# First unit of a chunked delta rule ahead of an MLP: scores times solved values directly behind T times v, corner products in pieces, SyncE's loads behind T

## The chip, the cores and the metric

The kernel runs on one core of a Trainium2 chip. The metric is the device time of one execution in microseconds; three executions were timed, and one more was profiled. PE is TensorE, DVE is VectorE, ACT is ScalarE, POOL is GpSimd, SP is SyncE, which here only issues DMAs.

## The reference

Two stages: a delta rule over 768 tokens for 4 batches and 8 heads (head size 48), then an MLP with a squared ReLU over the 3072 rows that it gives.

```
k_n = k / (norm(k) + 1e-6)
for t in range(S):
    y[:, :, t] = q_t @ state
    v_old = state^T k_t
    state = state + beta_t * outer(k_t, v_t - v_old)
x = y.transpose(0, 2, 1, 3).reshape(B * S, H * D)
out = square(max(x @ w_in, 0)) @ w_out        # 384 -> 2048 -> 384, float32
```

## The kernel before

**Units.** The 768 tokens are cut into 12 units of 64 tokens. A unit takes all 4 batches and 8 heads, two batches stacked on the 128 partitions (`NC = 2` such pairs). For a unit the recurrence becomes matrix products: the keys' own products below the diagonal, with beta, form a triangular system; its inverse is T (`ttile`, `tt`); solved values are T times v (`solved`, L632); the output is queries times state plus masked scores times solved values (`onward`, L660); the new state is the old one plus keys times solved values (L649). The first unit has no state yet, so its output is the scores' product alone and its state is a copy (L669).

**T of the first two units.** `invert_both` (L430) inverts for both units at once, DVE working through 15 steps on 16x16 corners (L446 to L454), two transposes (L459), then for unit x = 0 and x = 1 the off-diagonal 16x16 blocks by two rounds of small matmuls: L472, a copy to SBUF by ACT (L474), L479, a subtraction on DVE (L481). The next size, 32x32, follows in `whole` (L550, ACT L553, L558, ACT L560). Parts of T go to their place by DMAs (L497, half of them on ACT's queue, half on SP's for unit 0, all on SP's for unit 1). Inverses of later units run on DVE alone (L518, L519), spread over the unit before.

**The MLP.** `moe` (L671) transposes a unit's output (L680), splits it into a high and a low float32r part (ACT L683, DVE L684), and multiplies: L714 for the first product (nine matmuls for 128 of the 2048 columns), ACT L721, L722, L724 and DVE L693 for the squared ReLU and its split, L701 for the second.

**Weights.** 28 pieces w0 to w27 (128x512 of w_in or 128x384 of w_out) are loaded by SP (`fetch`, L127) and split on the chip into high and low parts: ACT scales (L141), DVE forms words (L149, L151, L153), ACT casts the high part (L159), PE and ACT make the low part (L166, L167, L168). The first `FIRST = 8` pieces do this with three matmuls and without DVE's L173; the later ones take a subtraction on DVE (L173) and two matmuls. A generator (`splits`) does a third of a piece at each `take`.

**What sets the order.** All five engines run in program order; nothing is scheduled behind the author's back. Ahead of the loop over units the order is written out by hand as calls of `take(generator, n)`. In the loop `weave` sorts pieces by tables of positions: 0 to 1 is one unit of MLP work, `CHAIN1` places unit 1's T, state and output, `corner` the rest of the joint inverse. PSUM tiles: x and h two banks each, g one pair, o0 and o1. DMAs on SP and ACT are issued in order, too: one that waits holds all behind it.

The queries of the first units pass through one buffer, `qpad` (L253 `load_q`, L345 transposes, L361 scores, L408 copies, L411 mask); keys are normalized in `normalize` (ACT L293, DVE L297 to L309).

Of the kernel before, what the change touches and what calls it, by code (L numbers as in the profile page):

```python
# [8 lines left out]
F32 = mybir.dt.float32  # L9
# [4 lines left out]
ALU = mybir.AluOpType  # L14
# [7 lines left out]
def kernel(  # L22
# [94 lines left out]
    AHEAD = 14  # L117
    FIRST = 8
    LAG = 3
# [310 lines left out]
    def invert_both():  # L430
# [32 lines left out]

        def quarters(u):
            ps = x_tile(u)[:, :H2 * QB].rearrange("p (h t) -> p h t", h=H2)
            return ps, [(h, n, slice(n * HB, (n + 1) * HB)) for h in range(H2) for n in range(4)]

        for x in range(2):
            nc.vector.transpose(out=turned[x], in_=parts[x])
            ps, places = quarters(2 * x)  # L470
            for h, n, q in places:
                nc.tensor.matmul(ps[q, h], lhsT=ds_[x]["ap"][q, h // H, h % H, 0, n % 2 * HB:(n % 2 + 1) * HB],  # L472
                                 rhs=parts[x][q, h, QB:], start=True, stop=True)
            nc.scalar.copy(out=mids[x], in_=ps)  # L474
            yield
            ps, places = quarters(2 * x)
            for h, n, q in places:
                low = slice(n * HB, n * HB + QB)
                nc.tensor.matmul(ps[q, h], lhsT=turned[x][low, h], rhs=mids[x][low, h], start=True, stop=True)  # L479
            yield  # L480
            nc.vector.tensor_tensor(out=parts[x][:, :, QB:], in0=parts[x][:, :, QB:], in1=ps, op=ALU.subtract)  # L481
            if x == 0:
                ds_[0]["t1"] = mpool.tile([P, H2, HB], F32, name="h_h", bufs=3)
                nc.vector.transpose(out=ds_[0]["t1"], in_=parts[0])
                ds_[0]["low"] = parts[0]
            else:
                nc.gpsimd.memset(ttile[1][:, :, :, :HB], 0.0)
                yield
                ds_[1]["t1t"] = t1t = apool.tile([P, H, HB], F32, name="t1t", bufs=1)
                for n in range(4):  # L490
                    up = n // 2 * C
                    nc.sync.dma_start(out=t1t[n * HB:(n + 1) * HB], in_=parts[1][up:up + HB, n % 2::2])
            rows = ttile[x].rearrange("p c h t -> p (c h) t")
            for n in range(4):
                q = slice(n * HB, (n + 1) * HB)
                queue = nc.sync if x or n % 2 else nc.scalar
                queue.dma_start(out=rows[q, :, n % 2 * HB:(n % 2 + 1) * HB], in_=parts[x][q])  # L497
            yield
# [137 lines left out]
    def onward(d):  # L636
# [3 lines left out]
        gy = areas([g[:, j] for j in range(2)], NP)  # L640
        if u < units - 1:
            ku = areas([x_tile(u) for _ in range(2)], NP)
# [8 lines left out]
            for b in range(2):  # L651
                for j in range(2 if u else 0):
                    rows = slice(j * C, j * C + D)
                    nc.vector.tensor_tensor(out=state[rows, b], in0=state[rows, b], in1=ku[b][rows], op=ALU.add)  # L654
        for c in range(NC):
            for h in range(H):
# [10 lines left out]
        if not u:  # L667
            for b in range(2):
                nc.vector.tensor_copy(out=state[:, b], in_=ku[b])  # L669

# [105 lines left out]
    def state_part(d):  # L776
        yield from whole(d)
        solved(d)
        yield
        onward(d)  # L780
        yield
# [3 lines left out]
    CHAIN = (14.9, 18.4, 21.9, 25.4)  # L785
    CHAIN1 = (14.4, 17, 19.5, 21.5, 23.5, 27)
    L1, N1 = [0.01], (0.36, 0.76)
# [8 lines left out]
    with tc.manual_schedule(engines=engines):  # L796
# [23 lines left out]
        lows(1)  # L820
        for x in range(4, 8):
            scaled(x < 7)
            worded(1)
            highs(1)
            lows(1)
        fetch(2)
        load_q(ds_[0])
        fetch(3)
        fetch(3)
        highs(1)  # L830
        lows(2)
        take(pair[0], 3)
        scaled(2)
        fetch(3)
        load_q(ds_[1])
        load_v(ds_[0])
# [4 lines left out]
        take(inverse, 1)  # L841
        take(splits, 2)
        take(inverse, 1)
        chain = state_part(ds_[0])
        take(chain, 1)
        fetch(3)
        ds_.append(load(2))
        fetch(NW)
        take(splits, 3)
        take(chain, 1)  # L850
        take(splits, 4)
        take(pair[0])
        take(chain, 1)
        take(pair[1], 2)
        take(splits, 3)
        take(chain, 1)
        take(splits, 1)
        first, third = moe(ds_[0]), normalize(ds_[2])
        take(first, 1)
        take(splits, 2)  # L860
        take(pair[1], 1)
# [6 lines left out]
        split_early = False  # L868
        used = 6 + 2 + 3 + 4 + 3 + 3 + 3
        before = None  # L870
        corner, inverse = inverse, None
        for u in range(1, units):
# [13 lines left out]
            if u == 1:  # L886
                parts.append((corner, [0.04, 0.09, 0.1]))
                parts.append((third, [0.01, 0.015, 0.03, 0.045]))
                parts.append((late_loads(), [0.08]))
                parts.append((splits, steps(3 * (NW - FIRST) + 3 - used, 0, 0.72)))  # L890
                parts.append((pair[1], [0.25]))
# [41 lines left out]
```

## Time and profile before

| | us |
|---|---|
| median of three executions | 626.48 |
| lowest, highest | 624.90, 628.03 |
| profiled execution, device time | 628.73 |
| its span in the profile | 627.0 |
| PE busy in it | 588.2 |
| mean granted clock of TensorE, share of 2.4 GHz | 0.963 |

The profile is one execution, 0.36% above the median of the three. Between the span and the device time lie 1.7 us. The page gives shares for the whole span; the change touches the first 115 us, so views of that stretch are what to read: waits of one engine, the timeline and busy time by stretches. A timeline row gives start, length, engine, line, operation and tiles; the bracket at its end is the idle time of that engine before it and what ended it.

### The profile page before, as it was taken

Reading aid. Unit: us, or ns where it says so; the run is one execution under the profiler, and the core shown is the slowest. Engines: PE = TensorE matmul, PEld = TensorE weight load, DVE = VectorE, ACT = ScalarE, POOL = GpSimd, SP = SyncE. Lnnn points to the kernel's source line nnn. Section 1 sums busy time; section 2 is a strip of 40 time slices with the busy share of each in tenths; the row PEclk is TensorE's granted clock in tenths of the full one; section 3 lists DMA queues with packets and bytes.
Section 4 is the critical chain, followed back from the end, with each engine's and each line's share of the span. In section 5 each row is a group of like instructions: output and inputs, shape, how many; then the busy total and the mean of one; then the engine's idle time right before and its main releaser. Section 6 shows DMA issues by size and latency. Waiting matters only on the chain.

```text
span 627.0 us, 23868 instructions
## 1 busy us (share of the span) xinstructions
PE 588.2 (94%) x10392; PEld 556.1 (89%) x10392; DVE 419.1 (67%) x1131; ACT 316.0 (50%) x621; POOL 29.4 (5%) x52
## 2 busy tenths in 40 slices
PE   2948688999999999999999999999999999999997
PEld 2536587899999999999999999999999999999996
DVE  4795769785795795794885875876866956931211
ACT  4845577455345435536446445454545444355442
POOL 4000010001001001001001000010010010000000
PEclk9955789799999999999999999999999999999999
DMA  7797736114427217317227226226234143030101
GB/s 225 200 284 158 203 59 108 20 28 80 81 40 118 56 28 119 61 29 123 53 40 116 52 44 112 53 45 104 53 59 90 27 80 68 3 69 2 26 1 26
DMA packets 172464, 49.32 MB, mean 79 GB/s; under 512 B 164288, under 2 KB 167368, under 8 KB 172360
## 3 DMA queue, kind: packets, MB, share of 16 engines
q1 hardware_dynamic: 168840, 47.06, 37.5%
q8 instruction: 82, 1.34, 0.9%
q10 hardware_dynamic: 3392, 0.72, 0.6%
q14 instruction: 22, 0.18, 0.1%
q0 software_dynamic: 128, 0.01, 0.0%
HBM read 36.54 MB, written 10.49 MB: 75 GB/s over the span
## 4 chain that ended last, share of the span: by engine, by line
PE 87%; ACT 3%; DMA 3%; DVE 2%; issue 2%; SPq 1%; ACTq 0%; DVEq 0%
PE o L701 33%; PE h L714 32%; PE x L361 2%; PE x L608 2%; PE g L608 2%; PE x L632 2%; PE g L660 2%; PE g L361 1%; PE x L649 1%; PE x L582 1%; PE x L345 1%; PE h L571 1%; PE h L680 1%; PE g L345 1%; DMA qpad<-in_q_dram 1%
## 5 line engine op out<-in xcount | busy, mean ns | idle before, releaser
L701 PE MATMUL o<-w,h_h 128*128 128x384 f32 x768 | 203.8, 347 | 0.0
L714 PE MATMUL h<-x_h,w 128*128 128x256 f32 x1152 | 171.2, 285 | 0.0
L721 ACT ACTIVATE r<-h 128x512 f32<-128x512 f32 x96 | 57.5, 599 | 223.6 <-PE h L714 223.5
L693 DVE TENSOR_TENSOR h_l<-r,h_h 128x512 fp32r<-128x512 f32 x96 | 67.9, 707 | 148.1 <-ACT h_h L724 146.7
L714 PEld LDWEIGHTS h<-x_h,w 128*128 128x128 f32 x1152 | 156.4, 191 | 1.2
L701 PEld LDWEIGHTS o<-w,h_h 128*128 128x128 f32 x768 | 134.6, 189 | 3.2
L701 PE MATMUL o<-w,h_l 128*128 128x384 f32 x384 | 130.1, 339 | 0.0
L518 DVE SCALAR_TENSOR_TENSOR tmp<-lt,bt,z 128x126 f32<-128x126 f32 (+22 forms) x310 | 95.8, 309 | 7.8
L714 PE MATMUL h<-x_l,w 128*128 128x256 f32 x576 | 100.1, 283 | 0.0
L519 DVE TENSOR_TENSOR z<-z,tmp 128x126 f32<-128x126 f32 (+22 forms) x310 | 79.2, 255 | 10.6
L714 PEld LDWEIGHTS h<-x_l,w 128*128 128x128 f32 x576 | 82.3, 190 | 0.0
L701 PEld LDWEIGHTS o<-w,h_l 128*128 128x128 f32 x384 | 72.5, 189 | 0.0
L722 ACT ACTIVATE r<-r 128x512 f32<-128x512 f32 x96 | 60.7, 633 | 3.1
L724 ACT CAST h_h<-r 128x512 fp32r<-128x512 f32 x96 | 59.5, 620 | 3.0
L507 POOL MEMSET z<- 128x512 f32 x10 | 5.3, 532 | 447.6 <-DMA inv<-z 368.9
L654 DVE TENSOR_TENSOR state<-state,x 48x384 f32<-48x384 f32 x40 | 22.0, 551 | 0.9 <-PE x L649 0.3
L361 PE MATMUL x<-kq 48*64 48x64 f32 (+1 forms) x608 | 19.1, 251 | 1.2 <-ACT kq L348 0.7
L361 PEld LDWEIGHTS x<-kq 48*64 48x64 f32 x608 | 16.6, 147 | 3.4 <-ACT kq L348 1.1
L345 PE MATMUL x<-plus,kpad 64*128 64x64 f32 x96 | 6.7, 240 | 12.4 <-DVE kpad L309 11.3
L586 ACT ACTIVATE tt<-x 32x256 f32<-32x256 f32 x44 | 16.4, 374 | 1.4 <-PE x L582 0.8
L345 PEld LDWEIGHTS x<-plus,kpad 64*128 64x128 f32 x96 | 5.4, 152 | 13.0 <-issue 12.8
L141 ACT ACTIVATE w<-w 128x384 f32<-128x384 f32 (+1 forms) x28 | 16.6, 615 | 0.0
(143 smaller groups left out, 635.8 us busy)
## 6 DMA issues: line engine op xcount, KB each, us to landing
w<-in_moe_w_in_dram SPq DMA_DIRECT2D x12, 512.0 KB
w<-in_moe_w_out_dram SPq DMA_DIRECT2D x16, 384.0 KB
lt<-blocks SPq DMA_DIRECT2D x20, 256.0 KB
qpad<-in_q_dram SPq DMA_DIRECT2D x96, 48.0 KB
vt<-in_v_dram SPq DMA_DIRECT2D x48, 96.0 KB
out_dram<-a SPq DMA_DIRECT2D x46, 96.0 KB
kpad<-in_k_dram SPq DMA_DIRECT2D x88, 48.0 KB
blocks<-ap SPq DMA_DIRECT2D x40, 64.0 KB
```

The costliest lines, as they stand in the source:

```text
L345: nc.tensor.transpose(pair[b][:, x, p], src[rows, c, 2 * p:2 * p + 2].rearrange("p a b -> p (a b)"), ident[rows, rows])
L361: nc.tensor.matmul(ps[j][to * C:(to + 1) * C, p, (x - first) * C:(x - first + m) * C], lhsT=kq[rows, c, p, b, 0], rhs=kq[rows, c, p, b, x: ...
L518: nc.vector.scalar_tensor_tensor(out=tmp, scalar=bt[:, s:s + 1], op0=ALU.mult, op1=ALU.mult, **factors)
L519: nc.vector.tensor_tensor(out=z[:, :nj, s + 1:], in0=z[:, :nj, s + 1:], in1=tmp, op=ALU.subtract)
L608: nc.tensor.matmul(dst[j][to, c, p], lhsT=d["kq"][rows, c, p, b, x], rhs=state[rows, b, c, p], start=(c == 0 and p == 0) if x else True, s ...
L654: nc.vector.tensor_tensor(out=state[rows, b], in0=state[rows, b], in1=ku[b][rows], op=ALU.add)
L693: nc.vector.tensor_tensor(out=h_l, in0=r, in1=h_h.bitcast(F32), op=ALU.subtract)
L701: nc.tensor.matmul(o[i], lhsT=a[:, e, i * P:(i + 1) * P], rhs=halves["wo", ft][w], start=(ft == 0 and n == 0), stop=(ft == FT - 1 and n == 2))
L714: nc.tensor.matmul(hp[:, e], lhsT=halves["wi", (kt, ft // EACH)][w][:, f], rhs=x[:, kt], start=(n == 0), stop=(n == 3 * KT - 1))
L721: nc.scalar.activation(out=r, in_=hp, func=AF.Relu)
L722: nc.scalar.activation(out=r, in_=r, func=AF.Square)
L724: nc.scalar.copy(out=h_h, in_=r)
```

## The change

- `FIRST` goes from 8 to 7: w7 is split by the later method, behind the joint inverse's steps on DVE and not ahead of them.
- SP's queue is written in another order: queries of unit 0 ahead of w8; only w8 to w12 and v ahead of the DMAs of T (L515 now, L497 before); w13 to w16, queries of unit 1, keys of unit 2 and w17 to w27 behind them. For unit 1 the DMAs of T come ahead of unit 3's keys (the loads' places are moved by the corner's earlier places).
- In `onward` the state of unit 0 (now `to_state`, L668 and L672) stands behind the output: T v, scores times solved values, the transposes of the output, then keys times solved values. Queries of unit 1 and one weight piece that stood between come behind, too.
- In `invert_both` the corner products of unit 1 are issued in four pieces of 32 matmuls (two rounds, two halves) and go to the g banks instead of x; the corner table has five places and not three. Unit 1's first chain places move by 0.8 and 0.1 of 32.

```diff
-    FIRST = 8
+    FIRST = 7
...
-        def quarters(u):
-            ps = x_tile(u)[:, :H2 * QB].rearrange("p (h t) -> p h t", h=H2)
-            return ps, [(h, n, slice(n * HB, (n + 1) * HB)) for h in range(H2) for n in range(4)]
+        def rounds(x, ps):
+
+            for g in range(1 + x):
+                for h in range(g * H, H2 if g == x else H):
+                    for n in range(4):
+                        q = slice(n * HB, (n + 1) * HB)
+                        yield h, n, q, ps[q, h]
+                if g < x:
+                    yield
...
+            if x:
+                two = ps_g.tile([P, 2, PC], F32, name="g")
+                two = [two[:, i] for i in range(2)]
+            else:
+                two = [x_tile(0) for _ in range(2)]
...
-        if u < units - 1:
+
+        def to_state():
...
             for b in range(2):
-                for j in range(2 if u else 0):
+                if not u:
+                    nc.vector.tensor_copy(out=state[:, b], in_=ku[b])
+                    continue
+                for j in range(2):
...
+        if 0 < u < units - 1:
+            to_state()
...
         if not u:
-            for b in range(2):
-                nc.vector.tensor_copy(out=state[:, b], in_=ku[b])
+            yield
+            to_state()
...
-    CHAIN1 = (14.4, 17, 19.5, 21.5, 23.5, 27)
+    CHAIN1 = (13.6, 17.1, 19.6, 21.6, 23.6, 27)
...
-        fetch(2)
         load_q(ds_[0])
-        fetch(3)
-        fetch(3)
+        fetch(5)
...
-        scaled(2)
-        fetch(3)
-        load_q(ds_[1])
         load_v(ds_[0])
...
-        take(splits, 2)
+        take(splits, 3)
         take(inverse, 1)
+        fetch(4)
+        load_q(ds_[1])
         chain = state_part(ds_[0])
         take(chain, 1)
-        fetch(3)
         ds_.append(load(2))
         fetch(NW)
...
-        take(splits, 4)
+        take(splits, 6)
...
-                parts.append((corner, [0.04, 0.09, 0.1]))
+                parts.append((corner, [0.02, 0.05, 0.065, 0.075, 0.085]))
```

SP's queue ahead of the DMAs of T (`tt`) and just behind them; `w_` with a number is a piece of the weights (before, w_417 is w8 and w_519 w18; after, w_413 is w8 and w_714 w13), `lt` the joint inverse's input. Before, where w8 and w9, queries (`qpad`) and w10 to w14 stand ahead of this:

```order
L127 DMA w_439<-in_moe_w_in_dram 128x1024
L127 DMA w_515<-in_moe_w_in_dram 128x1024
L127 DMA w_517<-in_moe_w_out_dram 128x768
L127 DMA w_519<-in_moe_w_out_dram 128x768
L253 DMA qpad<-in_q_dram 64x4x48 x8
L247 DMA vt<-in_v_dram 64x8x48 x4
L497 DMA tt_108<-lt 32x16x32 x2
L127 DMA w_779<-in_moe_w_out_dram 128x768
L127 DMA w_781<-in_moe_w_out_dram 128x768
```

and after, from the load of `lt` on:

```order
L386 DMA lt<-both 128x1024
L253 DMA qpad<-in_q_dram 64x4x48 x8
L127 DMA w_413<-in_moe_w_in_dram 128x1024
L127 DMA w_415<-in_moe_w_in_dram 128x1024
L127 DMA w_417<-in_moe_w_out_dram 128x768
L127 DMA w_419<-in_moe_w_out_dram 128x768
L127 DMA w_421<-in_moe_w_out_dram 128x768
L247 DMA vt<-in_v_dram 64x8x48 x4
L515 DMA tt_108<-lt 32x16x32 x2
L127 DMA w_714<-in_moe_w_out_dram 128x768
L127 DMA w_716<-in_moe_w_in_dram 128x1024
```

Between `lt` and T stood eleven pieces of weights and two sets of queries; now five pieces and one set do, and w13 to w16 stand directly behind T.

PE from T times v of unit 0 to the scores of unit 1 (L361; `o_` are banks for the low parts of weights). Before:

```order
L632 MATMUL h<-vt,tt_108 64x48 x32
L345 MATMUL x<-plus,qpad 128x64 x16
L166 MATMUL o_936<-w_815,plus 128x384
L167 MATMUL o_936<-h_l,plus 128x384
L649 MATMUL h<-vt,kpad_100 64x48 x32
L660 MATMUL g<-vt,ap 64x48 x32
L680 MATMUL h<-plus,y 128x64 x12
L166 MATMUL o_1042<-w_863,plus 128x384
L167 MATMUL o_1042<-rest,plus 128x384
L361 MATMUL x<-kq 64x64 x16
```

and after:

```order
L650 MATMUL h<-vt,tt_108 64x48 x32
L685 MATMUL g<-vt,ap 64x48 x32
L705 MATMUL h<-plus,y 128x64 x12
L668 MATMUL x<-vt,kpad_100 64x48 x32
L166 MATMUL o_1009<-w_850,plus 128x384
L167 MATMUL o_1009<-h_l,plus 128x384
L345 MATMUL h<-plus,qpad 128x64 x16
L166 MATMUL o_1042<-w_863,plus 128x384
L167 MATMUL o_1042<-rest,plus 128x384
L361 MATMUL x<-kq 64x64 x16
```

The same work; the output's product and its transposes go to the front, the state's product and unit 1's queries behind them.

ACT between the last piece of T (L560, now L578) and the copy of the solved values (L634, now L652). Before:

```order
L560 ACTIVATE tt_108<-x 32x16x32 x2
L168 CAST w_659<-o_853 128x512
L141 ACTIVATE w_437<-w_437 128x512
L159 CAST w_863<-a 128x384
L168 CAST w_733<-o_866 128x384
L634 COPY vt<-h 128x8x48 x2
```

and after:

```order
L578 ACTIVATE tt_108<-x 32x16x32 x2
L141 ACTIVATE w_714<-w_714 128x384
L159 CAST w_850<-r 128x384
L168 CAST w_700<-o_853 128x512
L141 ACTIVATE w_716<-w_716 128x512
L159 CAST w_863<-a 128x384
L168 CAST w_802<-o_866 128x384
L652 COPY vt<-h 128x8x48 x2
```

Six pieces of weight work stand there and not four; two of them (w_714, w_716) read pieces that SP loads behind T.

## Rows read from the trace of the kernel before

**Rows 1.** Busy time by stretches: stretch (us), its length, then busy us (and count) of PE, PEld, DVE, ACT, POOL, the granted clock as a share of 2.4 GHz, the DMA share and GB/s.

```profile
34.30:61.50 27.20, 18.61 (x552) 15.71 (x552) 21.02 (x49) 14.15 (x30) 0.53 (x1) 0.50 0.82 239
61.60:71.70 10.10, 7.02 (x337) 5.82 (x337) 5.91 (x13) 6.91 (x18) 0.00 (x0) 1.00 0.65 187
71.90:82.00 10.10, 8.04 (x155) 7.47 (x154) 8.27 (x18) 3.85 (x9) 2.21 (x3) 0.50 0.56 141
82.10:109.20 27.10, 22.66 (x310) 20.14 (x308) 21.65 (x44) 22.42 (x45) 0.00 (x0) 1.00 0.55 93
109.40:116.10 6.70, 6.16 (x74) 5.80 (x75) 5.72 (x20) 2.08 (x6) 0.00 (x0) 0.50 0.28 49
116.30:624.00 507.70, 505.87 (x8777) 488.05 (x8775) 335.09 (x935) 245.50 (x470) 18.88 (x27) 1.00 0.33 58
...
89.10:110.60 21.50, 17.97 (x291) 16.13 (x292) 20.36 (x40) 17.44 (x36) 0.00 (x0) 0.97 0.59 98
```

**Rows 2.** Waits of PE between 35 and 115 us: line, what it waited for, us in total, times, the longest.

```profile
PE x L479 <- issue: 5.5, 2, 3.5
...
PE g L660 <- issue: 2.0, 1, 2.0
```

**Rows 3.** Timeline of DVE around the start of the joint inverse.

```profile
28.53 0.43 DVE L149 TENSOR_SCALAR r<-w 128x512 int32<-128x512 int32 x1
...
30.25 0.69 DVE L446 TENSOR_TENSOR lt<-lt,bt 128x512 f32<-128x512 f32 x1
```

**Rows 4.** The source view of L446: its semaphore reads on DVE, ns shortest, middle and longest, and when.

```profile
L446 DVEq EVENT_SEMAPHORE  x4: 21/50/50, 29.5 to 30.2; - x4
```

**Rows 5.** Timeline of DVE and PE from the end of the joint steps to the subtraction for unit 0.

```profile
43.27 0.39 DVE L149 TENSOR_SCALAR a<-w 128x512 int32<-128x512 int32 x1
...
46.29 0.69 DVE L173 TENSOR_TENSOR w<-a,w 128x512 fp32r<-128x512 f32 x1
...
48.89 1.03 PE L479 MATMUL x<-t,h_h 16*32 16x16 f32 x60 [3.46 <-issue]
...
49.98 0.42 DVE L481 TENSOR_TENSOR lt<-lt,x 128x256 f32<-128x256 f32 x1 [1.13 <-PE x L479]
```

**Rows 6.** Timeline from T's DMAs to the copy of the solved values, unit 0.

```profile
52.95 2.67 SPq L497 DMA_DIRECT2D tt<-lt  x2
...
54.65 0.55 ACT L141 ACTIVATE w<-w 128x384 f32<-128x384 f32 x1
...
56.15 1.20 ACT L560 ACTIVATE tt<-x 32x512 f32<-32x512 f32 x2 [0.55 <-PE x L558]
...
57.29 8.49 SPq L253 DMA_DIRECT2D kpad<-in_k_dram  x8
...
57.83 1.96 PE L632 MATMUL h<-vt,tt 64*64 64x48 f32 x64
57.85 0.69 ACT L141 ACTIVATE w<-w 128x512 f32<-128x512 f32 x1
58.43 0.51 ACT L159 CAST w<-a 128x384 fp32r<-128x384 f32 x1
...
59.82 0.86 ACT L634 COPY vt<-h 128x384 f32<-128x384 f32 x2 [0.51 <-PE h L632]
```

**Rows 7.** Timeline from there to the MLP's input, unit 0.

```profile
59.72 1.12 PE L345 MATMUL x<-plus,qpad 64*128 64x64 f32 x16
...
60.87 1.07 ACT L348 COPY kq<-x 128x512 f32<-128x512 f32 x2 [0.18 <-PE x L345]
...
61.66 1.15 PE L649 MATMUL h<-vt,kpad 64*64 64x48 f32 x64
...
65.38 0.56 PE L660 MATMUL g<-vt,ap 64*64 64x48 f32 x24 [1.99 <-issue]
...
67.86 1.02 DVE L684 TENSOR_TENSOR x_l<-h,x_h 128x384 fp32r<-128x384 f32 x2 [2.40 <-ACT x_h L683]
```

**Rows 8.** Timeline from unit 2's norms to the second split of the hidden layer.

```profile
71.22 1.01 DVE L297 TENSOR_REDUCE n<-kq 128x8 f32<-128x384 f32 x2 [0.34 <-ACT kq L293]
...
71.81 1.47 PE L714 MATMUL h<-x_h,w 128*128 128x256 f32 x6
...
73.85 0.41 PE L479 MATMUL x<-t1t,z 16*32 16x16 f32 x14
...
76.31 1.73 PE L479 MATMUL x<-t1t,z 16*32 16x16 f32 x114 [2.06 <-issue]
...
77.00 0.96 DVE L309 TENSOR_TENSOR kpad<-kpad,s 128x768 f32<-128x768 f32 x1
...
83.88 0.58 ACT L168 CAST w<-x 128x512 fp32r<-128x512 f32 x1
...
84.28 0.69 PE L345 MATMUL x<-plus,kpad 64*128 64x64 f32 x8 [1.16 <-issue]
...
88.45 0.87 PE L714 MATMUL h<-x_h,w 128*128 128x256 f32 x6
...
89.11 0.69 DVE L693 TENSOR_TENSOR h_l<-r,h_h 128x512 fp32r<-128x512 f32 x1 [3.13 <-ACT h_h L724]
```

**Rows 9.** The chain of waits, the load of the first piece of weights: start, us from issue to landing, what.

```profile
6.79 3.46 DMA w<-in_moe_w_in_dram
```

**Rows 10.** The page's row on the queue that loads instructions: packets, MB, share of 16 engines.

```profile
q8 instruction: 82, 1.34, 0.9%
```

More of the change, by code (lines that the diff above doesn't have):

```diff
@@ L468, in invert_both @@
         for x in range(2):
             nc.vector.transpose(out=turned[x], in_=parts[x])
-            ps, places = quarters(2 * x)
-            for h, n, q in places:
-                nc.tensor.matmul(ps[q, h], lhsT=ds_[x]["ap"][q, h // H, h % H, 0, n % 2 * HB:(n % 2 + 1) * HB],
+            if x:
[3 more added lines that the diff above has]
+                two = [x_tile(0) for _ in range(2)]
+            two = [i[:, :H2 * QB].rearrange("p (h t) -> p h t", h=H2) for i in two]
@@ L473, in invert_both @@
+            for place in rounds(x, two[0]):
+                if not place:
+                    yield
+                    continue
+                h, n, q, to = place
+                nc.tensor.matmul(to, lhsT=ds_[x]["ap"][q, h // H, h % H, 0, n % 2 * HB:(n % 2 + 1) * HB],
                                  rhs=parts[x][q, h, QB:], start=True, stop=True)
-            nc.scalar.copy(out=mids[x], in_=ps)
+            nc.scalar.copy(out=mids[x], in_=two[0])
             yield
-            ps, places = quarters(2 * x)
@@ L477, in invert_both @@
-            for h, n, q in places:
+            for place in rounds(x, two[1]):
+                if not place:
+                    yield
+                    continue
+                h, n, q, to = place
                 low = slice(n * HB, n * HB + QB)
-                nc.tensor.matmul(ps[q, h], lhsT=turned[x][low, h], rhs=mids[x][low, h], start=True, stop=True)
+                nc.tensor.matmul(to, lhsT=turned[x][low, h], rhs=mids[x][low, h], start=True, stop=True)
             yield
-            nc.vector.tensor_tensor(out=parts[x][:, :, QB:], in0=parts[x][:, :, QB:], in1=ps, op=ALU.subtract)
+            nc.vector.tensor_tensor(out=parts[x][:, :, QB:], in0=parts[x][:, :, QB:], in1=two[1], op=ALU.subtract)
@@ L651, in onward @@
             for b in range(2):
-                for j in range(2 if u else 0):
+                if not u:
+                    nc.vector.tensor_copy(out=state[:, b], in_=ku[b])
+                    continue
+                for j in range(2):
                     rows = slice(j * C, j * C + D)
                     nc.vector.tensor_tensor(out=state[rows, b], in0=state[rows, b], in1=ku[b][rows], op=ALU.add)
+        if 0 < u < units - 1:
+            to_state()
         for c in range(NC):
@@ L667, in onward @@
         if not u:
-            for b in range(2):
-                nc.vector.tensor_copy(out=state[:, b], in_=ku[b])
+            yield
+            to_state()
     def moe(d):
@@ L779, in state_part @@
         yield
-        onward(d)
+        yield from onward(d)
         yield
@@ L820 @@
         lows(1)
-        for x in range(4, 8):
-            scaled(x < 7)
+        for x in range(4, 7):
+            scaled(1)
             worded(1)
@@ L850 @@
         take(chain, 1)
-        take(splits, 4)
+        take(splits, 6)
         take(pair[0])
         take(chain, 1)
+        take(splits, 1)
+        take(chain, 1)
+        first, third = moe(ds_[0]), normalize(ds_[2])
+        take(first, 1)
+        take(chain, 1)
+        take(splits, 2)
         take(pair[1], 2)
         take(splits, 3)
[L856 to L860, printed above, removed]
         take(pair[1], 1)
@@ L868 @@
         split_early = False
-        used = 6 + 2 + 3 + 4 + 3 + 3 + 3
+        used = 6 + 3 + 3 + 6 + 3 + 3 + 3
         before = None
```

## The prediction

> **What bounds the kernel now.** I read busy time by stretches first. From 116 us to the end PE is busy 505.87 of 507.70 us [rows 1]: no order of work ahead of 116 us changes that part, and a microsecond gained or lost before it moves the end by one. So the question is only when the stretch from 116 us begins. In it nothing is touched but places of unit 1.
>
> Before 116 us no single engine is full. Three things in the rows bind in turn. From 28 to 60 us it is the chain to T: joint steps on DVE, small products on PE, copies on ACT [rows 3, 5, 6]. From 60 to 89 us it is PE and ACT in turns, with two holes of PE inside a run of equal instructions that no other engine ended [rows 2, 7, 8], and a granted clock of 0.50 between 71.9 and 82.0 [rows 1]. From 89.1 to 110.6 us DVE is busy 20.36 of 21.50 us [rows 1], the rest being the few tens of ns between its many instructions: it is full there. DVE's last real hole ahead of it are the 3.13 us before the split at 89.11, when it waits for ACT and so for PE [rows 8]. This decides how a gain is to be counted: it counts if it brings forward the instant at which that split starts, and it then passes through DVE's full stretch one to one.
>
> **The change part by part.**
>
> *Step 1, the joint steps start sooner.* DVE is free of w6 at 28.53 and spends until 30.15 on w7's words before L446 [rows 3]. Without them it can start when `lt` has landed. The semaphore reads before L446 took at most 50 ns, the first at 29.5, so `lt` was there by then [rows 4]. The gain lies between 0.75 (30.25 less 29.5) and 1.7 us (28.53); with no row for the landing I take 1.35, about the middle.
>
> *Step 2, the subtraction for unit 0 (L481, now L499).* Before, DVE was done with its weight work at 48.85 and waited 1.13 us for PE, which stood 3.46 us on issue [rows 5]. Now DVE has three 512-column pieces (w7 to w9) and two remainders between the transposes and L499. Two pieces' words took 43.27 to 46.29, 1.5 each; a remainder 0.65 [rows 5]. From 43.3 less 1.35: 41.95 + 4.5 + 1.3 = 47.8. PE's products start 1.35 us sooner as well, and even with its whole stall they end at 48.6. So L499 starts at 47.8 to 48.6; I take 47.8, 2.2 sooner, since SP's loads have run dry by then (only five pieces instead of eleven are under way), and with them what I think held the fetch. From here w7 costs DVE 2.15 us of new work, and the stall on issue loses its victim: DVE is what is late.
>
> *Step 3, T to the solved values.* The order L481 to L560 stays, so L578 starts at 56.15 - 2.2 = 53.95 and ends at 55.15. SP's half of T's DMAs, which took until 55.62 to issue behind queries and v [rows 6], now wait for L499 alone: SP, with its shorter list out, stands idle until 48.3, and w13 to w27, queries of unit 1 and keys of unit 2 are queued behind that wait. ACT then has six pieces of weight work before the copy where it had four: 0.55 + 0.51 + 0.59 + 0.69 + 0.51 + 0.49 = 3.34 us (the first, second and fourth from [rows 6]; the others are of the same kinds). Copy of the solved values at 58.5 instead of 59.82: 1.3 sooner, of 2.2. T times v itself (1.96 us from 55.5 on) is ready a microsecond before that.
>
> *Step 4, the output first.* From the copy's end (59.35) the scores' product runs directly: 64 passes, 1.96 us by T times v at the low clock [rows 6], 1.15 by the state's product at the high one [rows 7]. I take the low one: 61.3. From the last of it (65.94) to `x_l` (68.88) the rows need 2.94 us [rows 7], so `x_l` is there at 64.25, 4.6 us sooner. What left the path: queries 1.12, one weight piece 0.8, the state's product 1.15, a hole of 1.99 [rows 7].
>
> *Step 5, where that gain goes.* The same work now stands behind: state 1.15 to 1.96, weight piece 0.8, queries 1.12, and ACT's copy of the transposed queries (1.07), which was hidden at 60.87 and now stands in front of the scores [rows 7]. Together 4.1 to 5.0 us against 4.6. ACT's scores and squares, and so DVE's norms of unit 2 (L297, 71.22), keep their time: between 0.5 sooner and 0.4 later; I take 0. The second round of unit 1's corner (L479, 73.85) needs the transposes that follow L297 on DVE and an ACT copy; it keeps its time, too.
>
> *Step 6, from there to unit 2's transposes (L345, 84.28).* Here the gain comes back. PE's work from 73.85 at the high clock: half a round 0.8, nine L714 1.3 (six took 0.87 [rows 8]), half a round 0.8, nine more 1.3, one low part 0.65, and 0.2 for changes between: 78.9. Before, it took until 83.1, with the 2.06 us hole and at 0.50, where six L714 take 1.47 [rows 1, 8]. DVE's side: norms end at 77.96 [rows 8], three operations on w17 1.4, ACT's cast 0.5 and its copy 0.6, which frees the bank that L345 needs (it did so at 84.46 [rows 8]): 80.5. The later of both is 80.6, so 84.28 moves by 3.7. The split at 89.11 follows to 85.4. DVE's own work ahead of it ended at 85.98 (89.11 less the hole of 3.13 [rows 8]); it has weight pieces in it that start sooner once ACT is ahead, so I expect it done by 85.4, and if it did not move at all the gain would be 3.1.
>
> *Where stalls on issue go.* They fell in the midst of runs of equal small passes: 60 of unit 0's second round, 114 of unit 1's and 24 of the scores' product were still to come [rows 5, 7, 8]. With halves of 64 passes between nine large matmuls that pattern is gone for unit 1; the hole of 1.99 would now fall in the state's product, which nobody on the path waits for. The queue that loads instructions moved 1.34 MB in 82 packets [rows 10]. The Trainium skill, "Runtime: NRT & Kernel Launch", section "Instruction fetch mechanics", says that instructions are refilled in blocks of 16 KiB and that crossing a block is mostly hidden; the packets' size agrees, the holes do not [rows 2]. By that rule the 2.06 us would have another cause and would stay, and PE would come to L345 at 81.0 instead of 80.6: the sum would be 3.3, not 3.7.
>
> *At no cost:* w7's third matmul goes, in a time when PE idles. Unit 1's T moves ahead of unit 3's keys on SP; PE's waits name neither. CHAIN1's shifts move L571 by half a step of dense PE work.
>
> **The sum.** 3.7 at L345, the same at the split of 89.11, the same at the end. The profiled execution would take 628.73 - 3.7 = 625.0; it stood 2.25 above the median, so the median goes from 626.48 to **622.8**.
>
> **The rivals.**
>
> *A: the clock stays at 1.2 GHz through the seventies.* For it: it fell at 71.8 after a stretch with 3 us of holes [rows 1], and after has a new hole of some 2 us (solved values' copy) just there. Against it: 61.3 to 80 has fewer holes than before. Step 6 at the low clock: 73.85 + 1.05 + 2.3 + 1.05 + 2.3 + 1.5 = 82.05, so 2.2 at L345, and some 1.4 more goes because L345 and what follows run slow until it rises. Gain 0.8: 625.7.
>
> *B: loads come late behind SP's wait.* w13 and w14 are issued at about 50; ACT needs w14 at 56.8. A lone piece landed 3.46 us after its issue [rows 9], so there are some 3 us to spare; w17 stands behind 16 small loads (eight took 8.49 with their waits [rows 6]), is issued at 62 to 67 and needed at about 72, which leaves 1 to 6. If landing takes 10 us, the solved values' copy slips by 3.4 and step 6 with it: gain 0.3, 626.2.
>
> *C: the clock rises early,* already with T times v. The scores' and state's products, the queries and scores take 2.1 us less in total, and all of step 5 with them: 5.7, 620.8.
>
> *D, slower: the clock is still 1.2 GHz when unit 2's transposes come.* Before, 82.1 to 109.2 ran at 1.00 with PE busy 22.66 us [rows 1]. If it stays low for 8 us more of that, PE needs some 4 us more, on top of A: 626.48 - 0.8 + 4 = 629.7. It decides at the clock of the stretch that begins with L345: at 1.00 there, D is out.
>
> **How the numbers follow.** Chances: forecast 0.47, A 0.23, B 0.12, C 0.10, D 0.08. The low-clock stretch at 109.4 to 116.1 may also come out longer or shorter; PE is busy 6.16 us in it, so half of that, 3 us, is all it can give, and I add 1.5 each way. The range reaches from C with none of this to A and B with it: 620.0 to 627.8. About 0.5%, 3.1 us, can be told from no change. Faster by more than that (under 623.35) are two thirds of the forecast and C: 0.41. Slower by more (over 629.6) is D and a tail of B: 0.10. The rest is 0.49.
>
> **What would show each step.** Step 1: L446 at 28.6 to 29.5. Step 2: L499 near 47.8 with DVE busy up to it. Step 3: the solved values' copy at 58.5, ACT busy before it, no wait of ACT L141 for a load. Step 4: no hole between T times v and the transposes but ACT's two copies, `x_l` near 64. Step 5: L297 near 71. Step 6: L345 of unit 2 near 80.6, no wait on issue over 1 us in the corner products, clock 1.00 from about 67 to 82. Then the split of 89.11 at 85.4 and DVE full for 21.5 us from it. I would be wrong if L345 keeps its 84 us, or if DVE shows holes in its full stretch, for then a gain at L345 does not pass through.

## The result and the profile after

The changed kernel takes **631.65 us** (median of 7 runs, 630.39 to 634.55) against 626.48 (7 runs, 624.35 to 628.37): ratio 1.0088, 95% interval 1.0060 to 1.0115. Forecast were 622.8 and a range from 620.0 to 627.8. Its profiled execution took 632.04 us with a span of 630.3, the one of before 628.73 and 627.0. So the profiles explain 3.3 us; the medians differ by 5.2, since the profile of before lay 2.25 above its own median and that of after 0.39 above its.

Steps 1 to 5 went as forecast or better. DVE after (start, length, line, operation, idle time ahead and what ended it):

```profile
28.92 0.69 DVE L446 TENSOR_TENSOR lt<-lt,bt 128x512 f32<-128x512 f32 x1 [1.05 <-DMA lt<-both]
...
47.98 0.41 DVE L499 TENSOR_TENSOR lt<-lt,x 128x256 f32<-128x256 f32 x1
...
61.89 1.02 DVE L709 TENSOR_TENSOR x_l<-h,x_h 128x384 fp32r<-128x384 f32 x2 [2.95 <-ACT x_h L708]
...
69.48 1.01 DVE L297 TENSOR_REDUCE n<-kq 128x8 f32<-128x384 f32 x2 [1.18 <-ACT kq L293]
...
91.06 0.69 DVE L718 TENSOR_TENSOR h_l<-r,h_h 128x512 fp32r<-128x512 f32 x1 [8.21 <-ACT h_h L749]
```

`x_l` (DVE L709) starts at 61.89 where 67.86 stood [rows 7], unit 2's norms (L297) are 1.7 us sooner, and then the split that was to come at 85.4 comes at 91.06, behind 8.21 us of waiting. That split stood at 89.11 before [rows 8]. The gain is lost between 77 and 91 us. PE there:

```profile
76.59 0.85 PE L739 MATMUL h<-x_h,w 128*128 128x256 f32 x5
80.07 0.38 PE L739 MATMUL h<-x_h,w 128*128 128x256 f32 x1 [2.62 <-issue]
...
81.71 0.37 PE L345 MATMUL x<-plus,kpad 64*128 64x64 f32 x1
82.45 0.69 PE L345 MATMUL x<-plus,kpad 64*128 64x64 f32 x7 [0.38 <-ACT w L168]
85.22 0.78 PE L345 MATMUL x<-plus,qpad 64*128 64x64 f32 x8 [2.08 <-DMA bt<-in_beta_dram]
```

Two waits stand there. PE stops for 2.62 us on issue, in the midst of nine large products. Then the transposes of unit 2's keys (`kpad`) run, and those of its **queries** (`qpad`) wait 2.08 us. The releaser that is named, `bt`, is the next load in the same queue; the chain of waits of after (start, length, what) shows what was late:

```profile
72.10 11.32 DMA w<-in_moe_w_out_dram
...
83.44 0.59 SPq L253
...
84.08 1.13 DMA bt<-in_beta_dram
...
85.22 0.78 PE x L345 x8
```

The last piece of weights took 11.32 us from issue to landing, and only then could SP issue the last of the eight loads of queries (L253), at 83.44: SP's loads go round eight semaphores, and this load uses the one of that piece, eight loads before it. SP after:

```profile
48.42 1.37 SPq L515 DMA_DIRECT2D tt<-lt  x2
...
52.98 7.40 SPq L253 DMA_DIRECT2D qpad<-in_q_dram  x8
60.43 5.80 SPq L253 DMA_DIRECT2D kpad<-in_k_dram  x8
66.68 1.77 SPq L127 DMA_DIRECT2D w<-in_moe_w_out_dram  x4
...
69.92 2.51 SPq L127 DMA_DIRECT2D w<-in_moe_w_out_dram  x4
74.43 9.61 SPq L253 DMA_DIRECT2D qpad<-in_q_dram  x8
```

and before:

```profile
70.15 8.07 SPq L253 DMA_DIRECT2D qpad<-in_q_dram  x8
```

Unit 2's queries are issued some 4 to 6 us later than before (the first at 74.43 against 70.15). Why, the stretches of after show (columns as in [rows 1]: PE, PEld, DVE, ACT, POOL, clock, DMA share, GB/s):

```profile
42.80:48.40 5.60, 3.32 (x130) 2.41 (x130) 5.43 (x11) 3.34 (x7) 0.00 (x0) 0.50 0.01 3
...
56.60:60.00 3.40, 1.87 (x88) 1.49 (x84) 2.21 (x4) 2.17 (x6) 0.00 (x0) 1.00 0.83 147
60.00:73.70 13.70, 13.32 (x300) 11.61 (x301) 9.91 (x22) 9.59 (x24) 0.00 (x0) 0.50 0.64 180
73.70:80.50 6.80, 4.18 (x147) 3.46 (x146) 6.37 (x15) 4.06 (x8) 2.28 (x3) 1.00 1.02 401
80.50:90.80 10.30, 7.84 (x54) 6.53 (x53) 1.03 (x2) 4.26 (x8) 0.00 (x0) 0.50 0.34 49
```

and two of them before:

```profile
42.80:48.40 5.60, 2.17 (x131) 1.95 (x127) 5.39 (x12) 2.19 (x5) 0.46 (x1) 0.50 0.96 300
...
73.70:80.50 6.80, 4.74 (x140) 4.25 (x139) 6.02 (x15) 1.29 (x3) 2.21 (x3) 0.50 0.56 120
```

While SP waits for T, nothing is loaded for 5.6 us: 3 GB/s where before 300 ran. What is not loaded then runs between 73.7 and 80.5, at 401 GB/s and full DMA engines, where before 120 ran. Behind that the granted clock is 0.50 (1.2 GHz) from 80.5 to 90.8, where from 82.1 it was 1.00 before [rows 1].

Further on, the first product behind unit 1's solved rows starts at 113.92 (111.89 before, +2.03), and one more hole, not there before, adds 1.29 at 211 us: together the 3.3 us of the two spans. PE after, waits from 130 to 300 us:

```profile
PE g L626 <- issue: 1.3, 1, 1.3
```

The split of 89.11 belongs to an execution 2.25 us above the median. Runs 7 and 10 below took as long as the kernel before by their medians; in their traces (623.81 and 626.72 us) it stands at 86.99 and 85.93. Run 7, then run 10:

```profile
86.99 0.69 DVE L700 TENSOR_TENSOR h_l<-r,h_h 128x512 fp32r<-128x512 f32 x1 [3.13 <-ACT h_h L731]
```

```profile
85.93 0.69 DVE L693 TENSOR_TENSOR h_l<-r,h_h 128x512 fp32r<-128x512 f32 x1 [3.13 <-ACT h_h L724]
```

So the 1.95 us from 89.11 to 91.06 probably understate the loss; that isn't shown, since no trace of before near its median was kept.

### The profile page after: what moved, and what is told of

It reads as the page before. It is cut to its first block, busy times and chain, and to the rows that moved or that the text cites. A ratio compares the mean times of both kernels' runs of the same rounds, so it can differ in the third digit from the quotient of the medians.

```text
span 630.3 us, 23865 instructions
## 1 busy us (share of the span) xinstructions
PE 591.2 (94%) x10390; PEld 558.7 (89%) x10390; DVE 418.1 (66%) x1132; ACT 316.6 (50%) x621; POOL 31.0 (5%) x52
## 4 chain that ended last, share of the span: by engine, by line
PE 83%; DMA 6%; DVE 3%; SPq 3%; ACT 2%; issue 1%; ACTq 0%; DVEq 0%
PE o L726 33%; PE h L739 32%; DMA w<-in_moe_w_out_dram 3%; PE x L626 2%; PE g L626 2%; PE x L650 2%; DMA w<-in_moe_w_in_dram 2%; PE x L361 2%; PE g L685 2%; PE g L361 1%; PE x L668 1%; PE x L600 1%; PE h L589 1%; SPq L253 1%; PE x L345 1%
## 5 line engine op out<-in xcount | busy, mean ns | idle before, releaser
L739 PE MATMUL h<-x_h,w 128*128 128x256 f32 x1152 | 171.5, 285 | 2.6 <-issue 2.6
L739 PEld LDWEIGHTS h<-x_h,w 128*128 128x128 f32 x1152 | 156.4, 191 | 4.0 <-issue 2.8
L739 PE MATMUL h<-x_l,w 128*128 128x256 f32 x576 | 100.3, 283 | 0.0
L739 PEld LDWEIGHTS h<-x_l,w 128*128 128x128 f32 x576 | 82.3, 190 | 0.1
L361 PE MATMUL x<-kq 48*64 48x64 f32 (+1 forms) x608 | 19.4, 255 | 0.7 <-ACT kq L348 0.7
L361 PEld LDWEIGHTS x<-kq 48*64 48x64 f32 x608 | 17.1, 152 | 2.9 <-ACT kq L348 1.6
L345 PE MATMUL x<-plus,kpad 64*128 64x64 f32 x96 | 7.1, 248 | 11.8 <-DVE kpad L309 11.5
L528 POOL TENSOR_SCALAR_AFFINE_SELECT z<-z 64x512 f32<-64x512 f32 x20 | 17.4, 871 | 1.3
```

The costliest lines, as they stand in the source:

```text
L361: nc.tensor.matmul(ps[j][to * C:(to + 1) * C, p, (x - first) * C:(x - first + m) * C], lhsT=kq[rows, c, p, b, 0], rhs=kq[rows, c, p, b, x: ...
L528: nc.gpsimd.affine_select(out=half, in_=half, pattern=[[nz, J], [-1, HB]], base=g, channel_multiplier=0, compare_op=ALU.not_equal, fill=1.0)
L739: nc.tensor.matmul(hp[:, e], lhsT=halves["wi", (kt, ft // EACH)][w][:, f], rhs=x[:, kt], start=(n == 0), stop=(n == 3 * KT - 1))
```

## The experiments

Every run is set against runs of the kernel before on the same chip. First the two theories. **LOADS**: the dry queue makes weights and unit 2's queries late, and that costs. **PE**: the new order of products brings the hole and the low clock by itself. The medians of before beside them were 626.20 us (runs 1 to 4), 626.87 (5 to 8) and 626.98 (9 to 12).

**1. The changed kernel with the loads of the kernel before.**

```
+        fetch(2)
         load_q(ds_[0])
-        fetch(5)
+        fetch(6)
...
+        fetch(3)
+        load_q(ds_[1])
         load_v(ds_[0])
...
-        fetch(4)
-        load_q(ds_[1])
...
+        fetch(3)
         ds_.append(load(2))
```

> The changed kernel with SyncE's loads in the order of the kernel before (eleven pieces and the queries of unit 1 ahead of v and of T's DMAs); all else as changed. Theory LOADS: the weights' queue no longer runs dry while SyncE waits for T, w27 lands about 5 us sooner, unit 2's queries are there when TensorE comes for them; the wait of 2.08 us ahead of their transposes is gone, and the time is 623 to 626.5 us. The output's part comes a microsecond or two later than in the changed kernel, since T's DMAs stand behind loads again. Theory PE: the new order of products on TensorE (output first, corner halves) makes the hole of 2.6 us and the low clock behind it by itself; the hole and the low clock stay, and the time is 629 us or more.

628.02 us, ratio 1.0029 (1.0007 to 1.0051). The wait for unit 2's queries is gone and most of the loss with it, but it ends above the range given (626.5) and below that of PE (629): some 1.8 us over before remain.

**2. The kernel before with the loads of the changed kernel,** the same edit the other way round.

> The kernel before with SyncE's loads in the order of the changed kernel (only w8 to w12 and v ahead of T's DMAs, the rest behind); all else as before. LOADS: w27 and unit 2's queries land some 5 us later (about 83 and 85 us), the transposes of the queries wait for them, and the time is 629 to 632 us although T itself comes sooner. PE: no more than the 1 to 2 us that T gains or the loads lose; 624.5 to 627.5 us.

631.42 us, ratio 1.0093 (1.0059 to 1.0128): the whole loss, from SP's order alone. The same gap in the loads stands in its stretches:

```profile
42.80:48.40 5.60, 2.40 (x136) 2.19 (x138) 5.39 (x12) 2.47 (x5) 0.00 (x0) 0.50 0.01 3
```

DVE's subtraction for unit 0 starts at 47.71 in it, as in the changed kernel (47.98) and 2.3 us sooner than before [rows 5]: the dry queue alone gives the whole of step 2's gain; w7 late alone gives 1.05 (run 10). What the late loads hold up first here is unit 1's queries (PE, waits from 56 to 100 us):

```profile
PE x L345 <- DMA qpad<-in_q_dram: 2.3, 1, 2.3
PE x L479 <- issue: 1.9, 1, 1.9
```

Its profiled execution is the fastest of its six, so where the rest of the 5.2 us stands can't be read from it. Unit 2's queries, for which LOADS expected the wait, are not waited for in it: the time came as LOADS had it, the wait at another load of the same queue.

**3. Unit 2's queries ahead of w21 to w27.**

```
-        fetch(NW)
+        fetch(4)
...
         load_q(ds_[2])
+        fetch(NW)
```

> The changed kernel with unit 2's queries ahead of w21 to w27 in SyncE's queue. LOADS: the queries land by about 78 us, the wait of 2.08 us is gone; w21 to w27 come half a microsecond each later, which is late for none that is needed before 83 us; with the hole of 2.6 us and the low clock behind it still there the gain is 2 to 3 us (628.5 to 630); if the hole goes as well, 625 to 627. PE: the wait goes but the time stays within 1 us of 631.6.

629.90 us, ratio 1.0065 (1.0037 to 1.0092): a quarter to a third of the loss comes back. The profiled execution (629.88) has no wait for queries and no hole at L739, and the split comes at 87.37, 3.7 us sooner than in the changed kernel. Most of that is lost again behind it, at the next load of the same queue: the keys of unit 3, which the change put behind unit 1's DMAs of T. DVE, then ACT:

```profile
87.37 0.69 DVE L718 TENSOR_TENSOR h_l<-r,h_h 128x512 fp32r<-128x512 f32 x1 [3.76 <-ACT h_h L749]
```

```profile
103.74 1.19 ACT L293 ACTIVATE y<-kpad 128x384 f32<-128x384 f32 x2 [2.15 <-DMA kpad<-in_k_dram]
```

The first product behind unit 1's solved rows starts at 112.24, 24.9 us behind the split, where it was 22.9 in the changed kernel and 22.8 before. The clock changed as well:

```profile
60.00:82.00 22.00, 21.42 (x458) 18.05 (x453) 16.22 (x34) 13.71 (x31) 2.62 (x3) 0.50 0.63 181
```

PE was busy 21.42 of 22 us and stayed at 1.2 GHz throughout.

**4. w13 to w16 ahead of v and T's DMAs** (`fetch(9)` in place of `fetch(5)`, no `fetch(4)` behind T).

> The changed kernel with w13 to w16 issued ahead of v and of T's DMAs (nine pieces in place of five there), so that the weights' queue does not run dry; queries of unit 1 and the rest stay behind T. LOADS: nearly all of the 5.6 us of an idle queue are used, the last piece lands near 79 us, the wait for unit 2's queries is gone; T is copied 1 us later at most; 623 to 627 us. PE: 629 us or more, with hole and low clock as in the changed kernel.

629.16 us, ratio 1.0045 (1.0023 to 1.0067): half of the loss comes back. That is PE's range (629 or more), not that of LOADS. The wait for queries is gone; holes of 1.25 us (L497) and 1.52 us (L739) on issue remain, and the hole of unit 0's second round is 2.57 us again, where it was 0.63 in the changed kernel.

**5 and 6. What a hole on issue is.** Number all of PE's records (weight loads, matmuls, semaphore reads) in order of start. In before and after, the holes of over half a microsecond that are put down to issue inside a run of equal products then stand behind records 962, 1729, 2241 and 961, 2498, 6849: at 193 or 194 over a multiple of 256. (The 1.16 us on issue ahead of L345 [rows 8] stand at the head of a run, at 212 over a multiple of 256, and are not among these; their cause is open.) The queue that loads instructions moves 16 KB at a time [rows 10], and 20,957 records by 82 packets are 256 each. To test it, products that nobody reads were put ahead of PE's first work.

```
+        spare = ps_o.tile([P, PC], F32, name="o0")
+        for _ in range(60):                      # 128 in the other run
+            nc.tensor.matmul(spare[:C, :C], lhsT=ident[:, :C], rhs=ident[:, :C], start=True, stop=True)
```

> The kernel before with 60 tiny passes (64x64, a product of constants that nobody reads) ahead of TensorE's first work, while it stands idle until 11.3 us; nothing else is changed. In the traces so far every hole of TensorE put down to issue stands behind instruction 194 + 256k of its stream. Theory BLOCK: a hole belongs to that number, where the next 16 KiB of instructions have not come yet; with 120 instructions more in front the hole of 3.46 us in the second round of unit 0 (instruction 962) falls ahead of that round, where TensorE waits anyway, and is gone there; those at 1730 and 2242 move 60 passes up and get smaller or larger with the work in the 256 instructions ahead. Time 0 to 3 us less: 623.5 to 626.5 us. Theory PLACE: the holes belong to the products in which they stand (their banks or operands): they stay in the 60th pass of the second round and in the scores' product, and the time stays within 0.5 us of the kernel before.

> The kernel before with 128 such tiny passes ahead of TensorE's first work, 256 instructions, one whole block. BLOCK: the holes stand where they stood before (3.46, 1.99 and 2.06 us within 0.7), since a whole block moves no boundary against the program; time within 1 us of the kernel before. A third possibility, that the early passes matter by themselves (the clock rises sooner for them), would show here as well as with 60 passes: then both are faster or slower by the same.

627.97 us (1.0034, 1.0011 to 1.0058) and 634.00 us (1.0120, 1.0092 to 1.0148). Both times were mis-forecast: such a product is two passes with a weight load each, four records and not two, and 128 of them kept PE busy from 3.3 to 20.9 us, in the way of its first real work. So 60 are 240 records: the end of a block falls 16 records, 8 passes, later in the program. The holes moved by exactly that, from behind 68 and 14 passes [rows 5, 8] to behind 76 and 22; the one in L660 is gone, and one of 0.71 us (L472) is new. PE with 60 products:

```profile
45.24 1.25 PE L479 MATMUL x<-t,h_h 16*32 16x16 f32 x76 [0.46 <-ACT t L474]
49.38 0.93 PE L479 MATMUL x<-t,h_h 16*32 16x16 f32 x52 [2.88 <-issue]
...
71.27 0.37 PE L479 MATMUL x<-t1t,z 16*32 16x16 f32 x22
74.60 1.10 PE L479 MATMUL x<-t1t,z 16*32 16x16 f32 x106 [2.96 <-issue]
```

128 products are two whole blocks, and two of the three holes stand where they stood, to the pass:

```profile
52.73 1.15 PE L479 MATMUL x<-t,h_h 16*32 16x16 f32 x68 [0.48 <-ACT t L474]
57.28 1.03 PE L479 MATMUL x<-t,h_h 16*32 16x16 f32 x60 [3.40 <-issue]
...
69.39 0.76 PE L660 MATMUL g<-vt,ap 64*64 64x48 f32 x40
72.07 0.56 PE L660 MATMUL g<-vt,ap 64*64 64x48 f32 x24 [1.92 <-issue]
```

3.40 and 1.92 us, against 3.46 and 1.99. (The third, in unit 1's second round, is gone; one of 1.07 us stands a block earlier.) BLOCK holds, PLACE has fallen: such a hole belongs to the end of a block of 256 instructions, whatever product stands there (in run 12 one leaves its product).

How long it is depends on the loads. From the crossing into one block until the next could be used, at the same place (records 706 to 962) in runs that differ in SP's order, with busy time by stretches of exactly that time. Before, loads running:

```profile
42.79:48.89 6.10, 2.17 (x131) 1.96 (x127) 5.85 (x12) 2.58 (x5) 0.47 (x1) 0.50 0.92 283
```

After, queue dry:

```profile
41.67:44.90 3.23, 2.12 (x145) 1.94 (x137) 3.09 (x7) 1.43 (x3) 0.53 (x1) 0.50 0.03 8
```

Before with the loads of after, dry:

```profile
41.63:44.77 3.14, 2.16 (x145) 1.95 (x137) 3.00 (x7) 0.99 (x2) 0.52 (x1) 0.50 0.04 9
```

After with w13 to w16 early, running again:

```profile
41.84:47.00 5.16, 2.11 (x144) 1.93 (x136) 4.96 (x11) 2.54 (x5) 0.49 (x1) 0.50 0.93 213
```

PE's work is the same 2.1 us in all four. The block takes 3.1 to 3.2 us with idle DMA engines and 5.2 to 6.1 with loads under way; what is over PE's work is the hole and some 0.5 us in which PE waits for a copy by ACT. SP's order alone switches it either way.

**7. Output first, alone,** on the kernel before (the edits of `onward` and of the calls behind it).

> The kernel before with one part of the change alone: the first unit's scores times solved values directly behind T times v, its state, queries of unit 1 and the weight piece behind the output; loads, first pieces and corner as before. By step 5 of the prediction the output comes some 4 us sooner and norms of unit 2 keep their time, so TensorE reaches the second round of the corner as before: 625.5 to 627 us. If the output first is worth what it brings forward, 622 to 624. If it costs (the transposes of unit 1's queries and their copy stand in front of the scores, low clock): 627.5 to 629.

626.80 us against 626.87, ratio 1.0004 (0.9984 to 1.0025): no change within some 1.3 us, as step 5 said.

**8. The changed kernel with the loads and the corner of before,** that is output first and w7 late.

> The changed kernel with the loads of the kernel before, and with the corner products as before too (whole rounds of 128 passes, x banks, three places in the table, the chain's places as before); the output first and seven early pieces stay. The run with the loads alone undone took 628.0 us, 1.8 over the kernel before. If the pieces of the corner cost that, 626 to 627; if they gain (no hole in the midst of a round), 629 to 630.5; if the output first or the later w7 costs it, 628 as with the pieces.

629.05 us, ratio 1.0048 (1.0024 to 1.0072). Beside run 1 (1.0029) the pieces are not told apart from whole rounds; they are not what costs.

**9. Output first and pieces, w7 early, loads of before,** the best candidate that these runs point to.

> The kernel before with two parts of the change: output first (626.8 us alone, no change) and unit 1's corner products in four pieces on the g banks; w7 early and loads as before. If the pieces spare the hole of 2 us in the second round without a loss elsewhere, 624 to 626; if the hole only moves to the next end of a block (256 instructions on, behind large products), 626 to 627.5; if the low clock comes with the pieces, 628 or more.

626.14 us, ratio 0.9997 (0.9977 to 1.0018): no better than before, at the lower end of what was expected if the hole only moves. In its trace it has done neither: 1.66 us on issue stand in a half round of the corner (L497, at 77.0), behind the same record, 2241.

**10. w7 late, alone** (`FIRST = 7`, the calls ahead of it one piece shorter, and two longer `take`s).

> The kernel before with one part alone: w7 split by the later method (FIRST = 7); order of loads, output and corner as before. By steps 1 and 2 of the prediction the joint steps start 1.35 us sooner and T gains up to 2.2: 624 to 626. If the loads that stand ahead of T hold T anyway, and DVE's 2.15 us for w7 come on top, 627 to 629 (the runs with w7 late and the loads of before took 628.0 and 629.05, the one with w7 early and the output first 626.8).

627.02 us, ratio 1.0013 (0.9992 to 1.0034). The joint steps start at 28.84, 1.4 us sooner than before [rows 3], as step 1 had it; the subtraction starts at 48.93, 1.05 sooner, since a hole of 3.65 us stands ahead of it. The time is at the lower end of the second range expected, and not told apart from before.

**11. Both mends of SP's queue** (runs 3 and 4 in one).

> The changed kernel with both mends of SyncE's queue: w13 to w16 issued ahead of v and T's DMAs, and unit 2's queries ahead of w21 to w27. The first alone gave 629.2, the second 629.9. If only the late queries and the dry queue cost, both go here: 626 to 628. If the stalls on issue behind the loads of the seventies and the low clock are what is left, they stay: 628.5 to 630.

629.65 us, ratio 1.0039 (1.0016 to 1.0062): by the median no more than w13 to w16 early alone. But the twelve executions fall into two groups, and each of the two cases expected has one: five took 625.9 to 627.8 us, at a mean granted clock of 0.962 to 0.972, and six took 630.1 to 631.5, at 0.948 to 0.955; one lies between. What parts them is open. The one profiled is the slowest (631.45). In it the queries are there, and the stall takes the place of the wait:

```profile
78.00 0.86 PE L739 MATMUL h<-x_h,w 128*128 128x256 f32 x5
82.17 0.58 PE L739 MATMUL h<-x_h,w 128*128 128x256 f32 x1 [3.32 <-issue]
...
85.30 0.74 PE L345 MATMUL x<-plus,qpad 64*128 64x64 f32 x8
```

**12. Half a block of passes ahead of the changed kernel** (32 products, 128 records).

> The changed kernel with 32 tiny passes that nobody reads ahead of TensorE's first work: 128 instructions, half a block (a pass of this kind counts four in the stream, as the run with 60 of them showed). BLOCK: the hole of 2.62 us leaves the large products of L739 and stands about 64 passes earlier, in the half round of L497 ahead of them; the hole of 1.29 us at 211 us is gone. TensorE comes to unit 2's transposes at about the same time, and the queries land at 85 to 86 us as before, so the wait for them stays at 1.5 to 4 us: 629.5 to 631.5 us, the gain being the hole at 211. If the hole in L739 was what cost, and not the queries, 627 to 629.

632.17 us, ratio 1.0085 (1.0058 to 1.0112), a little over the range and the same as the changed kernel. The hole left L739 and stands in the half round ahead of it:

```profile
77.18 0.24 PE L497 MATMUL g<-t1t,z 16*32 16x16 f32 x5
79.98 0.68 PE L497 MATMUL g<-t1t,z 16*32 16x16 f32 x59 [2.57 <-issue]
...
84.90 0.85 PE L345 MATMUL x<-plus,qpad 64*128 64x64 f32 x8 [0.29 <-DMA qpad<-in_q_dram]
```

The hole at 211 us is gone, and others of 1.60 us (L685) and 1.12 us (at 166 us) came. The wait for queries is down to 0.29 and they start at 84.90 against 85.22: in the traces of runs 11 and 12, either of the hole and the late queries fills the room that the other leaves. Run 3 without both shows what they held up: 3.7 us at the split.

## Why the prediction was wrong

**Steps 1 to 5 held, or erred on the safe side.** L446 at 28.92 (28.9 forecast, the middle of a range since no row gave the landing of `lt`); L499 at 47.98 (47.8); `x_l` there at 62.91 (64.25: the copy of the solved values came at 57.75 and not 58.5, and the scores' product took 1.51 us and not 1.96, with the clock at 1.00 from 56.6 to 60.0). Step 5's norms of unit 2 came at 69.48, 1.7 us sooner than its 71.22 and outside its half microsecond; unit 1's second round kept its time (74.03 against 73.85). In step 2 the size was right and half of the reason: "their loads have run dry by then" did shorten the stall, to 0.63 us, but it was taken as a gift.

**Step 6 failed, by a wait that step 3 had written down and put no price on.** Step 3 says that w13 to w27, queries and keys are queued behind SP's wait for T; the sum then takes all of them as on time. Step 6 asked when PE and the ACT copy are ready for L345 and found 80.6. PE's side was right: 81.71 less the hole of 2.62 is 79.1, against 78.9. What it left out is the third thing that L345 needs, the queries, last in SP's queue behind w27. They were to be transposed at 81.05 (84.75 in the trace of before, less 3.7) and were at 85.22: 4.17 us late. From there to the split took 5.84 us, against 4.36 before (89.11 less 84.75), at a clock of 0.50: 1.48 more. 4.17 and 1.48 are the 5.65 by which 91.06 misses 85.4. The 4.17 are the hole and the queries together; which of them costs how much alone the runs don't part. What follows the split carried it on, as forecast, and the hole at 211 us came on top.

**Rival B named the mechanism and mis-sized it.** It priced lateness at w14 and w17, where ACT needs them, found 1 to 6 us to spare, and gave 0.12 and 626.2. ACT indeed hardly waited for weights (0.16 us for w13, 0.15 for w17). But after 5.6 us without loads what stood behind came late down to the tail, the queries of unit 2, which had no slack. Undoing the order alone brought the loss from 5.2 to 1.8 us (run 1), making it alone cost 5.2 (run 2): that SP's order costs is shown both ways.

**Stalls on issue inside a run do not belong to small products,** as the prediction had it ("with halves between nine large matmuls that pattern is gone"). They stand at every 256th instruction whose block is late, and last as long as it is. In the changed kernel this one stands behind the fifth of nine large products, and at 2.62 us it is longer than the 2.06 of before. Not because the block came later: from the crossing into the block ahead it took 5.92 us, against 6.11. PE was through with that block's work sooner, in 3.30 us against 4.05, at a clock of 1.00. After, then before:

```profile
74.15:80.07 5.92, 3.30 (x143) 2.91 (x139) 5.53 (x13) 3.61 (x7) 2.28 (x3) 1.00 1.02 408
```

```profile
70.20:76.31 6.11, 4.05 (x151) 3.64 (x140) 5.53 (x13) 4.21 (x12) 0.00 (x0) 0.63 1.02 317
```

The Trainium skill, "Runtime: NRT & Kernel Launch", section "Instruction fetch mechanics", gives blocks of 16 KiB, 256 instructions, which runs 5, 6 and 12 bear out, and says that crossing one is mostly hidden. Measurements differ there: here it was hidden only where PE took longer than 3 us (5 to 7 with loads running) for the block before. The rival cause that the prediction drew from that rule for the 2.06 us is refuted, but so is the forecast that they go.

**Rivals A and C did not decide:** the clock was 1.00 from 56.6 to 60.0, 0.50 from there to 73.7 and 1.00 again to 80.5, and PE still came within 0.2 us of step 6's time but for the hole. **Rival D's condition came true** (clock 0.50 when L345 starts, 80.5 to 90.8), at 1.48 us up to the split and not 4; its 629.7 lies nearest to the time measured, but most of the loss has another cause. Run 3 is A's case: clock 0.50 up to 82, and L345 at 82.02, where A has 82.05. Whether the hole of 2.62 us brought the clock down is not settled: in run 3 it stayed at 0.50 with PE busy 97% and no hole.

**Two smaller terms.** Under "at no cost" stands that unit 1's T moves ahead of unit 3's keys, since PE's waits name neither. ACT reads those keys, and in run 3 it waited 2.15 us for them; in the changed kernel it didn't. And the range's lower end, 620.0, is 0.8 below C's 620.8, from which it was said to be taken.

**The rest of the change brings nothing that can be measured.** Output first alone is 0 (run 7), the pieces on top of it 0 (run 9), w7 late alone 0 (run 10), each within some 1.3 us. With w7 late on top of them it is 0.3 to 0.4% slower (run 1 against run 9, run 8 against run 7); the intervals of each pair touch or overlap, so that w7 costs is likely and not shown. So even without the loads the gain of 3.7 us would not have come (run 1 still lies 1.8 us over before).

## What to carry to other kernels

A wait put into a DMA queue can cost at any load behind it, down to the last that the queue owes: find the consumer and the slack of each, not of the next load alone. Here it was unit 2's queries in the changed kernel, unit 1's queries in run 2 and unit 3's keys in run 3. Before calling a stall on issue a property of some products, number the engine's instructions: the holes here that stood at a fixed remainder of 256 were late blocks, and moved with instructions added ahead of them. Of each instant that a sum rests on, list all its inputs with the queue that each comes by.

## What the runs showed of the hardware

- A block of 256 PE instructions was ready 3.0 to 3.2 us after the block before it was entered with idle DMA engines (3.9 in run 12, at 13 GB/s), and 5.1 to 6.8 us after with weights loading; in the MLP later on holes appeared at 3.5 to 4.4 us.
- A small float32 product (L479, and those put in) counted as two passes and four instructions, so 64 of them are a whole block.
- The granted clock stayed at 0.50 for 22 us with PE busy 21.42 us (run 3), and was 1.00 for 6.8 us with PE busy 4.18 (after, 73.7 to 80.5).
- Single executions of one kernel spread over 7 us (before: 622.75 to 630.15 over all runs), and run 10, level with before by its median, has the split of 89.11 at 85.93, so one profile is no measure of an effect of 0.5%.
